# Where TensorE's and ScalarE's hardware loops begin, and where P·V of the last pair stands, in a two-layer decode kernel

## The chip, the cores and the metric

The kernel runs on one core of a Trainium2 chip. A core has TensorE (PE in the profile: matmuls, with the weight loads as a row of their own, PEld), VectorE (DVE), ScalarE (ACT), GpSimd (POOL), and SyncE (SP), which here only starts transfers. Each engine runs its own list of instructions in order and waits on semaphores that the others raise. 16 DMA engines move data from the device's memory (HBM) into the core's on-chip memory (SBUF). TensorE writes to another on-chip memory, PSUM, which the other engines read.

The metric is the device time of one execution in microseconds, the median of several runs.

## The reference, cut to what matters

Two sequences (B = 2) decode one token each. Two layers run one after the other with the same weights and caches: attention A with a residual, then a small MLP block B with a residual.

```python
def _A_ref(x, k_cache, v_cache, wq, wo):          # x: (2, 1, 576), after a layer norm
    q = (x @ wq).reshape(2, 1, 32, 128).transpose(0, 2, 1, 3)
    scores = einsum("bhqd,bhkd->bhqk", q, k_cache) * 128 ** -0.5   # k_cache: (2, 32, 16384, 128)
    p = softmax(scores)
    o = einsum("bhqk,bhkd->bhqd", p, v_cache)
    return o.transpose(0, 2, 1, 3).reshape(2, 1, 4096) @ wo
def _B_ref(x, w1, w2, w3, w4):                    # one token each
    hs = ...      # gelu(layernorm(x) @ w1), shifted along the sequence of length 1, @ w2
    x1 = x + hs
    return x1 + gelu(layernorm(x1) @ w3) @ w4     # 576 -> 4608 -> 576
x = x + A(layernorm(x));  x = x + B(layernorm(x))      # layer 0
x = x + A(layernorm(x));  x = x + B(layernorm(x))      # layer 1
```

All inputs are bf16. For each of the 64 (sequence, head) units, K and V are 16384 x 128 numbers each, 4.2 MB; all of them are 537 MB, and the two layers read them nearly twice over. Nothing is reused within a layer, since each unit has one query.

## The kernel before, in words

**Tiles.** A unit's K lies in SBUF as 128 partitions x 128 rows of 128 numbers. TensorE can only contract over partitions, so half of K is transposed on it: eight 128x128 transposes make a chunk (into one of four PSUM buffers `tps`), ScalarE copies ("evacuates") the chunk into one of three SBUF buffers `kt`, and eight matmuls of two columns give its scores in the PSUM bank `sps`. VectorE does the other half without transposing: it multiplies 16 rows per partition by q, which has been spread over all partitions (`qb`), and sums over the 128 numbers ("a dot": TENSOR_TENSOR, then TENSOR_REDUCE).

**Pairs and singles.** Most units are handled two at a time. `pair` takes one transfer of 8.4 MB ("kk", K of two units, unit 0 on partitions 0 to 63, unit 1 on 64 to 127): 16 chunks on TensorE and ScalarE (`turned`, `evacuate`, `score`; scores trail the transposes by LEAD = 2 chunks), and 8 dots on VectorE beside them. A few units at the start and end of a layer are handled alone by `single` (8 chunks, 4 dots). Layer 0 has 1 single, 30 pairs (of which the last 29 are turns of a hardware loop), 3 singles; layer 1 has three units carried over in SBUF (`carried`), 1 single, 29 pairs (28 turns in the loop), 2 singles.

**q's broadcast.** `pair_diag` (VectorE) writes q of each unit onto a diagonal; `pair_q` multiplies that by a matrix of ones on TensorE and copies the result, q on every partition, to `qb[1]` (two ScalarE copies). They are done for the next pair at the end of a pair; `q_broadcast` is the same for a single.

**The end of a pair.** After the last scores VectorE takes the maxima (three short steps), GpSimd reduces over partitions (L1198), ScalarE scales the maximum and computes four exponentials into the tile `both` (L1201, L1206). In the next pair, after all of its 16 chunks, `pair_pv` multiplies V (a transfer "vv" of 8.4 MB) by these: 256 matmuls on TensorE (L1260), then ScalarE copies the result into `o_acc` (L1264). `pair_l`, behind chunk 8, sums the exponentials.

**What sets the order.** The order on each engine is the order in which the Python code emits operations; `Graph` works out the waits. GpSimd also passes landings on: a `relay` waits on GpSimd's queue for a transfer (POOLq L208 in the profile) and then raises a semaphore for TensorE or VectorE. Since that queue is in order, a relay also waits for GpSimd work ahead of it.

**The loop.** `attention` marks the position of TensorE, ScalarE and VectorE before the second pair, and `Graph.loop` turns everything from there into a hardware loop. So before the change all three engines' bodies run from the first chunk of a pair to the end of that pair. The first pair stands in front of the loop as straight code.

**Transfers.** SP issues them in one order (the store's plan) and waits until the buffer is free. In the loops there are two buffers for kk and one for vv: kk0, kk1, vv0, kk2, vv1, kk3, vv2 and so on. kk(i+2) waits until kk(i) is no longer read; its last reader on TensorE is `pair_q` of that pair, which takes the keys of K for this purpose (`self.pair_q(keys)`). vv(i) waits for ScalarE's copy of `pair_pv` of pair i-1. Since SP goes in order, kk(i+2) also stands behind vv(i).

**Around the loop's start.** `attention` calls `single` with a function `ahead`, which `single` runs at its chunk 0: the diagonals and `pair_q` of the first pair and the broadcast for the first single behind the loop (unit `leave`). After that single's softmax and P·V, GpSimd clears the upper half of `both` (L1019), which pairs need to be zero there. Then come the relays of kk0.

Of the kernel before, what the change touches and what calls it, by code (L numbers as in the profile page):

```python
# [32 lines left out]
class Graph:  # L33
# [74 lines left out]
    def mark(self):  # L108
        return {e: len(self.ops[e]) for e in self.LOOPED}

    def loop(self, first, turns, shift):

        for e, i in first.items():
            self.shift[e][i] = shift
            n = len(self.ops[e]) - i
            assert n % turns == 0, (e, n, turns)
            self.loops[e][i] = (n // turns, turns)

# [218 lines left out]
class KB:  # L337
# [15 lines left out]
    LEAVE = (61, 62)  # L353
    KK = ((0, 2), (0, 4))
    VV = (4, 2)
    TURNS = {("w3", 0): 1, ("w3", 1): 1, ("w3", 2): 1, ("w4", 1): 1, ("w4", 3): 1, ("w4", 6): 1, ("w4", 8): 1,
             ("wq", 0): 1, ("wq", 1): 1, ("wq", 2): 1}

# [637 lines left out]
    def attention(self, l):  # L996
        U = self.U
        self.l_now = l
        o = self.order(l)
        enter, leave = self.ENTER[l], self.LEAVE[l]  # L1000
# [6 lines left out]
        def ahead():  # L1007
            self.pair_diag(o[enter])
            self.pair_q()
            self.pair_column(o[enter])  # L1010
            self.q_broadcast(o[leave], leave, 2)
        self.single(l, s, ahead)
        self.softmax_max(l, s, o[s])
        self.softmax_exp(l, s, o[s])
        self.landed(l, "v", o[s])
        for g in range(4):
            self.pv(l, s, o[s], g)
        self.keep_by_act(l, s)
        self.pool(lambda e: e.memset(self.both[64:, 0, :], 0.0), writes=[*self.both_keys, "cleared"])  # L1019
        firsts = [o[s] for s in range(enter, leave, 2)]  # L1020
        for i, u in enumerate(firsts):
            if i == 1:
                first = self.g.mark()
                self.base = self.chunk
            self.pair(l, i, u, firsts[i - 1] if i else None)
        a, z = self.KK[l]
        self.g.loop(first, len(firsts) - 1, (z - a) * self.TILE // 2)
        self.base = None
        if l == 0:
            self.single(l, leave, lambda: self.q_broadcast(o[leave + 1], leave + 1, 1, [("qb", 1)]))  # L1030
# [23 lines left out]
        u = o[U - 1]  # L1054
# [15 lines left out]
        c = self.place(l, s)  # L1070
        at = 4 * c
        o = self.mps[:, 448:449]
# [4 lines left out]
        i = (self.U - 2) % self.NS  # L1077
# [10 lines left out]
    def single(self, l, s, ahead, top=None, exp=None, pv=None, turn=False):  # L1088
# [4 lines left out]
        for c in range(2 * n):  # L1093
# [6 lines left out]
            self.chunk += 1  # L1100
            while len(pend) > self.LEAD:
                self.scores(*pend.pop(0))
            if c == 0:
                ahead()
            if c % n in (0, 2):
                i = c % n // 2
# [15 lines left out]
    def pair(self, l, i, u, was):  # L1122
# [46 lines left out]
        for c in range(n):  # L1169
            turned(c, self.chunk)  # L1170
            self.evacuate(c, self.chunk)
            pend.append((c, self.chunk))
            self.chunk += 1
            while len(pend) > self.LEAD:
                score(*pend.pop(0))
            if c % 2 == 0:
                dot(c // 2)
            if c == n // 2 and was is not None:
                self.pair_l(was)
        while pend:  # L1180
            score(*pend.pop(0))
        if was is not None:
            self.pair_pv(was)
        self.pair_q(keys)
        self.used(l, nm, 2 * NB)
        m0, m1 = self.mx2[:, 0:1], self.mx2[:, 1:2]
# [7 lines left out]
        for h, (lo, hi) in enumerate(sides):  # L1194
            self.dv(lambda e, h=h, lo=lo, hi=hi: e.tensor_tensor(out=self.mx2[lo:hi, 2 + h:3 + h], in0=m0[lo:hi],  # L1195
                                                                in1=m1[lo:hi], op=ALU.max),
                    reads=["mx2_0", "mx2_1"], writes=["mx2_2"], sig=("mx2", h))
        self.pool(lambda e: e.partition_all_reduce(self.mx2[:, 4:6], self.mx2[:, 2:4], channels=128, reduce_op=ROP.max),  # L1198
                  reads=["mx2_2", "cleared"], writes=["mx2_4"])
        self.pair_column(u + 2)  # L1200
# [2 lines left out]
        for part in (1, 0):  # L1203
            for h, (lo, hi) in enumerate(sides):
# [3 lines left out]
                    bias=self.mx2[lo:hi, 6 + h:7 + h], scale=self.scale, accum_out=self.ls2[lo:hi, part:part + 1]),  # L1208
                    reads=["mx2_6"] + ([("s_dve", 0), ("s_dve", 1)] if part else [("sps", 0)]),
                    writes=[*self.side[h][part], ("lsp", part, h)], sig=("exp", part, h))  # L1210

    def half_scores(self, h):

# [474 lines left out]
```

## Time and profile before

| | us |
|---|---|
| median of 3 runs | 2564.79 (2562.66 to 2565.45) |
| the profiled execution, its own time | 2565.86 |
| its span in the trace | 2564.1 |
| busy: DVE / PE / ACT / POOL | 1903.5 / 1646.0 / 1229.4 / 31.4 |
| HBM read | 1092.37 MB, 426 GB/s over the span |

The page of the profile gives busy time by engine, the span in 40 slices, the transfers by queue, the chain of waits that ended last, and the costliest groups of instructions. Other views are the timeline (instructions in order of time: start, length, engine, line, operation, tiles written and read, count, and in brackets the idle time of that engine before it and what ended it; "issue" is a wait for nothing that the profile shows), and a table by stretches of time (busy time of each engine, TensorE's granted clock, the share of time that the 16 DMA engines were busy, and GB/s). Neighbouring rows of the timeline overlap, since matmuls are pipelined.

### The profile page before, as it was taken

The numbers are of one execution on the slowest core, as the hardware profiler recorded it, in microseconds if no ns is written. First come the engines' busy times: TensorE is split into PE (matmuls) and PEld (weight loads), VectorE is DVE, ScalarE is ACT, GpSimd is POOL, SyncE is SP. The second block draws the span as 40 slices with busy tenths as digits, with TensorE's granted clock in tenths as the row PEclk, the third lists the DMA queues.
The fourth block names the chain that finished last, engine by engine and source line by source line (L and its number), as shares of the span: only waits on it lengthen the run. The fifth ranks groups of instructions, "written<-read, shape, count | busy, mean of one in ns | idle before, by whom it ended". The sixth has DMA issues, their size and how long they took to land.

```text
span 2564.1 us, 82334 instructions
## 1 busy us (share of the span) xinstructions
PE 1646.0 (64%) x34410; PEld 1441.1 (56%) x34410; DVE 1903.5 (74%) x1697; ACT 1229.4 (48%) x1943; POOL 31.4 (1%) x97
## 2 busy tenths in 40 slices
PE   3666576576575575675775775675665665665765
PEld 3555565465565565564665665565555555555655
DVE  4987787787787787788447887777877877877882
ACT  2545355355455454454434554454454454454551
POOL 0000000000000000000000000000000000000000
PEclk8676676676676676676656676676676776676765
DMA  9899999999999999999999899999999999999999
GB/s 413 372 430 440 427 440 427 440 427 440 427 440 427 440 427 440 427 440 419 407 408 419 359 441 426 441 426 441 426 441 426 441 426 441 426 441 426 441 426 384
DMA packets 29942, 1093.30 MB, mean 426 GB/s; under 512 B 3252, under 2 KB 4408, under 8 KB 10552
## 3 DMA queue, kind: packets, MB, share of 16 engines
q1 hardware_dynamic: 29880, 1092.39, 99.0%
q8 instruction: 49, 0.80, 0.1%
q14 instruction: 13, 0.11, 0.0%
HBM read 1092.37 MB, written 0.00 MB: 426 GB/s over the span
## 4 chain that ended last, share of the span: by engine, by line
DMA 73%; PE 18%; issue 6%; ACT 1%; SPq 1%; another core or an unknown queue 0%; DVE 0%; POOL 0%; ACTq 0%; POOLq 0%
DMA mem<-in_A_v_cache_dram 70%; PE mps L1260 16%; DMA mem<-in_B_w_dram 1%; SPq L103 1%; DMA mem<-in_A_k_cache_dram 1%; ACT kt L1466 1%; PE tps L1142 0%; ACT o_acc L1264 0%; PE mps L1588 0%; DMA mem<-in_A_wq_dram 0%; PE sps L1480 0%; DMA mem<-in_A_wo_dram 0%; PE tps L1451 0%; PE mps L919 0%
## 5 line engine op out<-in xcount | busy, mean ns | idle before, releaser
L1142 PE MATMUL tps<-same,mem 128*128 128x128 bf16 x7552 | 948.1, 244 | 575.7 <-POOLq L208 572.0
L1466 ACT ACTIVATE kt<-tps 128x1024 bf16<-128x1024 bf16 x992 | 969.4, 1033 | 358.1 <-PE tps L1142 329.4
L1142 PEld LDWEIGHTS tps<-same,mem 128*128 (+1 forms) x7552 | 688.0, 99 | 745.5 <-issue 583.1
L1167 DVE TENSOR_REDUCE s_dve<-prod 128x16 f32<-128x2048 bf16 x472 | 1078.4, 2285 | 14.2
L1162 DVE TENSOR_TENSOR prod<-mem,qb 128x2048 bf16<-128x2048 bf16 x472 | 578.0, 1224 | 472.7 <-POOLq L208 412.5
L1260 PE MATMUL mps<-both,mem 128*128 128x2 bf16 x15104 | 412.2, 165 | 67.2 <-POOLq L208 62.2
L1260 PEld LDWEIGHTS mps<-both,mem 128*128 128x128 bf16 x15104 | 407.3, 103 | 72.1 <-POOLq L208 67.0
L1153 PE MATMUL sps<-q_col,kt 128*128 128x2 bf16 x7552 | 329.0, 165 | 46.6 <-ACT kt L1466 41.9
L1153 PEld LDWEIGHTS sps<-q_col,kt 128*128 128x128 bf16 x7552 | 289.9, 98 | 60.4 <-ACT kt L1466 46.3
L1264 ACT ACTIVATE o_acc<-mps 128x2 f32 (+1 forms) x59 | 10.2, 173 | 509.0 <-PE mps L1260 509.0
L1201 ACT ACTIVATE mx_<-mx_ 128x2 f32<-128x2 f32 x59 | 12.0, 203 | 169.4 <-POOL mx_ L1198 169.4
L1234 ACT ACTIVATE qb<-sps 64x128 bf16<-64x128 f32 x122 | 33.1, 272 | 123.2 <-PE sps L1228 121.2
L1228 PE MATMUL sps<-diag,same 128*128 128x128 bf16 x61 | 17.6, 288 | 111.6 <-DVE p L1220 111.6
L1451 PE MATMUL tps<-same,mem 128*128 128x128 bf16 x640 | 69.3, 284 | 11.4 <-POOLq L208 11.0
L1498 DVE TENSOR_REDUCE s_dve<-prod 128x16 f32<-128x2048 bf16 x32 | 73.1, 2286 | 1.1
L1228 PEld LDWEIGHTS sps<-diag,same 128*128 128x128 bf16 x61 | 6.4, 106 | 116.4 <-DVE p L1220 116.4
L1451 PEld LDWEIGHTS tps<-same,mem 128*128 128x128 bf16 x640 | 56.1, 130 | 11.8 <-POOLq L208 11.7
L1206 ACT ACTIVATE both<-s_dve,mx_ 64x128 bf16<-64x128 f32 x118 | 47.0, 399 | 2.7
L1198 POOL PARTITION_ALL_REDUCE mx_<-mx_ x59 | 21.0, 355 | 2229.8 <-DVE mx_ L1195 2229.8
L1206 ACT ACTIVATE both<-sps,mx_ 64x128 bf16<-64x128 f32 x118 | 42.8, 362 | 2.3
L1466 ACT ACTIVATE mem<-tps 128x1024 bf16<-128x1024 bf16 x32 | 31.1, 1047 | 19.4 <-PE tps L1451 17.1
L1247 ACT ACTIVATE l<-ls_ 64x1 f32 (+1 forms) x118 | 34.5, 292 | 9.0
(154 smaller groups left out, 545.5 us busy)
## 6 DMA issues: line engine op xcount, KB each, us to landing
mem<-in_A_k_cache_dram SPq DMA_DIRECT2D x6, 4096.0 KB, 39.4
mem<-in_A_v_cache_dram SPq DMA_DIRECT2D x5, 4096.0 KB, 29.2
mem<-in_B_w_dram SPq DMA_DIRECT2D x21, 576.0 KB, 7.7
mem<-in_B_w_dram SPq DMA_DIRECT2D x7, 1152.0 KB, 33.0
mem<-in_A_v_cache_dram SPq DMA_DIRECT2D x3, 2048.0 KB, 44.9
mem<-in_A_wq_dram SPq DMA_DIRECT2D x10, 512.0 KB, 7.0
mem<-in_A_wo_dram SPq DMA_DIRECT2D x8, 576.0 KB, 14.9
mem<-in_A_wq_dram SPq DMA_DIRECT2D x4, 1024.0 KB, 8.0
```

The lines of the kernel that those rows point to most:

```text
L103: sp.dma_start(dst, src).then_inc(h, 16)
L1142: ins = pe.transpose(self.tps[t][:, j * 128:(j + 1) * 128], place(c * CH + j, 1), self.ident[:, :])
L1153: ins = pe.matmul(self.sps[0][:, 2 * b:2 * b + 2], lhsT=kt[:, j * 128:(j + 1) * 128], rhs=self.q_col2[:, :], start=True, stop=True, skip_g ...
L1162: self.dv(lambda e: e.tensor_tensor(out=prod, in0=place(NB + i * DB, DB).rearrange("p (j d) -> p j d", d=128), in1=qbc, op=ALU.mult), read ...
L1167: self.dv(lambda e: e.tensor_reduce(out=self.s_dve2[:, i * DB:(i + 1) * DB], in_=prod, axis=AX.X, op=ALU.add), reads=["prod"], writes=[("s ...
L1206: self.act(lambda e, h=h, lo=lo, hi=hi, src=src, part=part: e.activation(out=self.both[lo:hi, h, NB * part:NB * (part + 1)], in_=src, func ...
L1234: self.act(lambda e, h=h, lo=lo, hi=hi: e.activation(out=self.qb[1][lo:hi, :], in_=qps[lo:hi, 128 * h:128 * (h + 1)], func=ACT.Copy), read ...
L1247: self.act(lambda e, c, lo=lo, hi=hi: e.activation(out=self.l[lo:hi, bass.ds(c, 1)], in_=self.ls2[lo:hi, 0:1], func=ACT.Identity, bias=sel ...
L1260: ins = pe.matmul(self.mps[:, 448:450], lhsT=buf[:, b * 128:(b + 1) * 128], rhs=self.both[:, :, b], start=b == 0, stop=b == 2 * self.NB - ...
L1451: ins = pe.transpose(self.tps[t][:, j * 128:(j + 1) * 128], buf[:, j * 128:(j + 1) * 128], self.ident[:, :])
L1466: self.act(lambda e: e.activation(out=out, in_=self.tps[t][:, :], func=ACT.Copy), reads=[("tps", t)], writes=keys, sig=("evac", c, t, k))
L1498: self.dv(lambda e: e.tensor_reduce(out=sd[:, c0:c0 + DB], in_=prod, axis=AX.X, op=ALU.add), reads=["prod"], writes=[("s_dve", r)], sig=(" ...
```

## The change

Four things are changed; what is computed stays the same, and so does each engine's number of operations.

1. `pair` now returns marks, and `Graph.loop` takes an end as well as a start. VectorE's loop keeps its place. The loops of TensorE and ScalarE begin ahead of `pair_q` (q's broadcast for the next pair), so that a turn runs from the end of pair i-1 (broadcast, scaling of the maximum, exponentials) through the chunks of pair i. The number of turns stays 29 and 28; the end of the last pair is straight code behind the loop.
2. `pair_pv` of the pair before is called behind chunk 12 (PVAT, the 13th of 16), no longer behind the last scores. It takes ScalarE's copy into `o_acc` along.
3. In `single`, `ahead` runs at chunk 4 (`c == n`) instead of chunk 0, in all singles that have one. The broadcast for unit `leave` is taken out of `ahead` and stands behind the whole single.
4. GpSimd's clearing of `both` moves from ahead of the first pair into it, right before that pair's reduction over partitions (only where there is no pair before: `was is None`).

ScalarE around the loop of layer 0, before: copies of chunks into `kt` are L1466, q's copies L1234, the scaling and exponentials L1201 and L1206, `o_acc` L1264; the two L261 rows are the loop's head, REGISTER_ALU and COMPARE_AND_BRANCH its end.

```order
L1466 ACTIVATE kt<-tps 128x1024 x16
L1234 ACTIVATE qb<-sps 64x128 x2
L1201 ACTIVATE mx_<-mx_ 128x2
L1206 ACTIVATE both,ls_<-s_dve,mx_ 64x128 x2
L1206 ACTIVATE both,ls_<-sps,mx_ 64x128 x2
L261 ISA
L261 UNCONDITIONAL_BRANCH
L1466 ACTIVATE kt<-tps 128x1024 x9
```

And now, from the first pair's copies on (line numbers are 3 or 4 higher):

```order
L1470 ACTIVATE kt<-tps 128x1024 x16
L261 ISA
L261 UNCONDITIONAL_BRANCH
L1238 ACTIVATE qb<-sps 64x128 x2
L1204 ACTIVATE mx_<-mx_ 128x2
L1209 ACTIVATE both,ls_<-s_dve,mx_ 64x128 x2
L1209 ACTIVATE both,ls_<-sps,mx_ 64x128 x2
L1470 ACTIVATE kt<-tps 128x1024 x9
```

The loop's head has moved ahead of q's copies. Further down in the same turn ScalarE now has

```order
L1470 ACTIVATE kt<-tps 128x1024 x4
L1268 REGISTER_ALU
L1268 ACTIVATE o_acc<-mps 128x2
L1470 ACTIVATE kt<-tps 128x1024 x3
L261 REGISTER_ALU
L261 COMPARE_AND_BRANCH
```

so the copy into `o_acc` stands behind 13 chunks instead of 16, and the turn ends with three chunks.

TensorE at the end of a turn of layer 0, before (L1153 scores, L1260 P·V, L1228 q's broadcast):

```order
L1153 MATMUL sps<-q_col,kt 128x2 x24
L1260 MATMUL mps<-both,mem 128x2 x256
L1228 MATMUL sps<-diag,same 128x128
L1228 MATMUL sps<-p,same 128x128
L261 REGISTER_ALU
L261 COMPARE_AND_BRANCH
```

And now P·V (L1264) inside the turn, between the scores of chunk 10 and the transposes of chunk 13:

```order
L1142 MATMUL tps<-same,mem 128x128
L1153 MATMUL sps<-q_col,kt 128x2 x8
L1264 MATMUL mps<-both,mem 128x2 x256
L1142 ISA
L1142 MATMUL tps<-same,mem 128x128
```

So three chunks' transposes and five chunks' scores now stand behind P·V. VectorE in the single of layer 1 ahead of the loop, before (L1512 is the last step of the carried units; L1220, L1240, L1407 and L1414 write diagonals and columns of q, L1494 and L1498 are a dot):

```order
L1512 TENSOR_TENSOR mx<-mx 128x1
L1220 TENSOR_SCALAR diag<-same,q_f 128x128
L1220 TENSOR_SCALAR p<-same,q_f 128x128
L1240 CAST q_col<-q_f 128x2
L1407 CAST q_col<-q_f 128x1
L1414 TENSOR_SCALAR diag<-same,q_f 128x128
L1494 TENSOR_TENSOR prod<-mem,both 128x2048
L1498 TENSOR_REDUCE s_dve<-prod 128x16
```

And now:

```order
L1516 TENSOR_TENSOR mx<-mx 128x1
L1498 TENSOR_TENSOR prod<-mem,both 128x2048
L1502 TENSOR_REDUCE s_dve<-prod 128x16
L1498 TENSOR_TENSOR prod<-mem,both 128x2048
L1502 TENSOR_REDUCE s_dve<-prod 128x16
L1224 TENSOR_SCALAR diag<-same,q_f 128x128
L1224 TENSOR_SCALAR p<-same,q_f 128x128
L1244 CAST q_col<-q_f 128x2
```

Two of the single's four dots now stand ahead of the diagonals, and the second diagonal (for `leave`) comes after all four. The diff:

```diff
@@ -108,11 +108,11 @@
     def mark(self):
         return {e: len(self.ops[e]) for e in self.LOOPED}
 
-    def loop(self, first, turns, shift):
+    def loop(self, first, last, turns, shift):
 
         for e, i in first.items():
             self.shift[e][i] = shift
-            n = len(self.ops[e]) - i
+            n = last[e] - i
             assert n % turns == 0, (e, n, turns)
             self.loops[e][i] = (n // turns, turns)
 
@@ -353,6 +353,7 @@
     LEAVE = (61, 62)
     KK = ((0, 2), (0, 4))
     VV = (4, 2)
+    PVAT = 12
     TURNS = {("w3", 0): 1, ("w3", 1): 1, ("w3", 2): 1, ("w4", 1): 1, ("w4", 3): 1, ("w4", 6): 1, ("w4", 8): 1,
              ("wq", 0): 1, ("wq", 1): 1, ("wq", 2): 1}
 
@@ -1008,23 +1009,22 @@
             self.pair_diag(o[enter])
             self.pair_q()
             self.pair_column(o[enter])
-            self.q_broadcast(o[leave], leave, 2)
         self.single(l, s, ahead)
+        self.q_broadcast(o[leave], leave, 2)
         self.softmax_max(l, s, o[s])
         self.softmax_exp(l, s, o[s])
         self.landed(l, "v", o[s])
         for g in range(4):
             self.pv(l, s, o[s], g)
         self.keep_by_act(l, s)
-        self.pool(lambda e: e.memset(self.both[64:, 0, :], 0.0), writes=[*self.both_keys, "cleared"])
+        marks = []
         firsts = [o[s] for s in range(enter, leave, 2)]
         for i, u in enumerate(firsts):
             if i == 1:
-                first = self.g.mark()
                 self.base = self.chunk
-            self.pair(l, i, u, firsts[i - 1] if i else None)
+            marks.append(self.pair(l, i, u, firsts[i - 1] if i else None))
         a, z = self.KK[l]
-        self.g.loop(first, len(firsts) - 1, (z - a) * self.TILE // 2)
+        self.g.loop(marks[0], marks[-1], len(firsts) - 1, (z - a) * self.TILE // 2)
         self.base = None
         if l == 0:
             self.single(l, leave, lambda: self.q_broadcast(o[leave + 1], leave + 1, 1, [("qb", 1)]))
@@ -1100,7 +1100,7 @@
             self.chunk += 1
             while len(pend) > self.LEAD:
                 self.scores(*pend.pop(0))
-            if c == 0:
+            if c == n:
                 ahead()
             if c % n in (0, 2):
                 i = c % n // 2
@@ -1177,10 +1177,11 @@
                 dot(c // 2)
             if c == n // 2 and was is not None:
                 self.pair_l(was)
+            if c == self.PVAT and was is not None:
+                self.pair_pv(was)
         while pend:
             score(*pend.pop(0))
-        if was is not None:
-            self.pair_pv(was)
+        mark = self.g.mark()
         self.pair_q(keys)
         self.used(l, nm, 2 * NB)
         m0, m1 = self.mx2[:, 0:1], self.mx2[:, 1:2]
@@ -1195,6 +1196,8 @@
             self.dv(lambda e, h=h, lo=lo, hi=hi: e.tensor_tensor(out=self.mx2[lo:hi, 2 + h:3 + h], in0=m0[lo:hi],
                                                                 in1=m1[lo:hi], op=ALU.max),
                     reads=["mx2_0", "mx2_1"], writes=["mx2_2"], sig=("mx2", h))
+        if was is None:
+            self.pool(lambda e: e.memset(self.both[64:, 0, :], 0.0), writes=[*self.both_keys, "cleared"])
         self.pool(lambda e: e.partition_all_reduce(self.mx2[:, 4:6], self.mx2[:, 2:4], channels=128, reduce_op=ROP.max),
                   reads=["mx2_2", "cleared"], writes=["mx2_4"])
         self.pair_column(u + 2)
@@ -1208,6 +1211,7 @@
                     bias=self.mx2[lo:hi, 6 + h:7 + h], scale=self.scale, accum_out=self.ls2[lo:hi, part:part + 1]),
                     reads=["mx2_6"] + ([("s_dve", 0), ("s_dve", 1)] if part else [("sps", 0)]),
                     writes=[*self.side[h][part], ("lsp", part, h)], sig=("exp", part, h))
+        return {**self.g.mark(), "tensor": mark["tensor"], "scalar": mark["scalar"]}
 
     def half_scores(self, h):
 
```

## The prediction

> **What bounds the kernel now.** I read the page first, then a table of long and short stretches, then SP's rows and the timeline where the transfers pause. The page:
>
> ```profile
> span 2564.1 us, 82334 instructions
> ...
> q1 hardware_dynamic: 29880, 1092.39, 99.0%
> q8 instruction: 49, 0.80, 0.1%
> ```
>
> The transfers' packets fill 99% of 16 engines' time; no compute engine is near that. So an edit pays only where the DMA engines pause. Stretches (columns: length, then busy time and count of PE, PEld, DVE, ACT, POOL, TensorE's clock, DMA share, GB/s):
>
> ```profile
> 100.00:150.00 50.00, 43.37 (x948) 37.97 (x947) 44.99 (x36) 30.46 (x44) 0.35 (x1) 0.74 0.84 355
> 240.00:1180.00 940.00, 610.67 (x12479) 529.20 (x12480) 723.99 (x582) 467.15 (x729) 8.51 (x24) 0.68 1.00 433
> 1400.00:1450.00 50.00, 36.67 (x661) 31.71 (x662) 46.49 (x41) 30.17 (x51) 0.74 (x2) 0.64 0.78 323
> 1500.00:2430.00 930.00, 601.81 (x12373) 522.25 (x12370) 714.84 (x577) 457.99 (x720) 8.50 (x24) 0.68 1.00 433
> ```
>
> Within the loops the DMA share is 1.00 at 433 GB/s: a transfer of 8.39 MB takes 19.4 us, a pair's two 38.7 us, and nothing can be gained there. At each loop's start a hole is left: 0.16 x 50 = 8.0 us in layer 0 and 0.22 x 50 = 11.0 us in layer 1 (each to about 0.3, from the rounding of the share). 19.0 us is the most that filling both can give.
>
> Why the DMA engines pause: SP has nothing to issue. Layer 0, the second pair, which is the loop's first turn:
>
> ```profile
> 84.38 0.33 SPq L103 DMA_DIRECT2D mem<-in_A_k_cache_dram  x1
> ...
> 84.49 0.58 ACT L1234 ACTIVATE qb<-sps 64x128 bf16<-64x128 f32 x2 [11.44 <-PE sps L1228]
> ...
> 87.69 3.23 PE L1142 MATMUL tps<-same,mem 128*128 128x128 bf16 x24 [3.23 <-POOLq L208]
> ...
> 89.91 0.19 ACT L1206 ACTIVATION_READ_ACCUMULATOR both<-sps,mx_ 64x1 f32 x1
> ...
> 95.72 8.88 ACT L1466 ACTIVATE kt<-tps 128x1024 bf16<-128x1024 bf16 x9 [5.62 <-issue]
> ...
> 110.25 0.23 PE L1142 MATMUL tps<-same,mem 128*128 128x128 bf16 x1 [1.64 <-issue]
> ...
> 114.13 6.97 PE L1260 MATMUL mps<-both,mem 128*128 128x2 bf16 x256
> ...
> 121.21 0.17 ACT L1264 ACTIVATE o_acc<-mps 128x2 f32 x1 [7.37 <-PE mps L1260]
> ...
> 121.41 0.33 SPq L103 DMA_DIRECT2D mem<-in_A_v_cache_dram  x1
> ```
>
> kk2 goes out at 84.38; the next issue, vv1, is at 121.41, 0.20 us behind ScalarE's copy of the first pair's P·V. What was queued at 84.38 (vv0 and kk2) has run out by then. Two waits "issue" lie in this chain: 5.62 us at ScalarE's entry into the loop, 1.64 on TensorE in the middle of chunk 13. Nobody signals them. Behind the first row the Trainium skill, "Runtime: NRT & Kernel Launch", section on instruction fetch, says that a taken branch to code outside the window must fetch it first; that agrees with 5.62 us at the branch.
>
> Layer 1, the same place:
>
> ```profile
> 1403.64 0.33 SPq L103 DMA_DIRECT2D mem<-in_A_k_cache_dram  x1
> ...
> 1406.92 3.32 PE L1142 MATMUL tps<-same,mem 128*128 128x128 bf16 x24 [3.21 <-POOLq L208]
> ...
> 1409.36 8.75 ACT L1466 ACTIVATE kt<-tps 128x1024 bf16<-128x1024 bf16 x9
> ...
> 1421.08 0.34 PE L1153 MATMUL sps<-q_col,kt 128*128 128x2 bf16 x8
> ...
> 1423.56 0.23 PE L1142 MATMUL tps<-same,mem 128*128 128x128 bf16 x1 [1.41 <-issue]
> ...
> 1427.43 6.97 PE L1260 MATMUL mps<-both,mem 128*128 128x2 bf16 x256
> ...
> 1434.71 0.33 SPq L103 DMA_DIRECT2D mem<-in_A_v_cache_dram  x1
> ```
>
> Here ScalarE enters without a stall, and vv1 is still late, at 1434.71. The cause lies earlier, in the single ahead of the loop:
>
> ```profile
> 1356.24 0.25 DVE L1414 TENSOR_SCALAR diag<-same,q_f 128x128 bf16<-128x128 bf16 x1 [8.39 <-PE sps L1228]
> ...
> 1366.04 0.35 PE L1480 MATMUL sps<-q_col,kt 128*128 128x1 bf16 x8 [0.56 <-ACT kt L1466]
> ...
> 1370.86 0.21 DVE L1509 TENSOR_REDUCE mx<-sps 128x1 f32<-128x64 f32 x1
> ...
> 1371.36 0.35 POOL L1514 PARTITION_ALL_REDUCE mx<-mx  x1 [26.52 <-DVE mx L1512]
> ...
> 1376.41 0.31 POOL L1019 MEMSET both<- 64x256 bf16 x1 [4.70 <-PE mps L1588]
> ...
> 1376.52 1.23 DVE L1162 TENSOR_TENSOR prod<-mem,qb 128x2048 bf16<-128x2048 bf16 x1 [5.26 <-POOLq L208]
> ```
>
> VectorE stood 8.39 us before the second diagonal, because `diag` was still to be read by TensorE, which was busy with carried units; so its dots ended 4.5 us behind the last scores (1366.39). Then GpSimd's clearing waited 4.70 us for the single's P·V, and the relay of kk0 behind it let VectorE start the first pair only at 1376.52.
>
> **The change, part by part.**
>
> Loops begun ahead of q's broadcast. ScalarE has nothing to do for 11.44 us before 84.49, when its last chunk of the first pair is done. The branch now falls there, so its 5.62 us lie in that idle time. If ScalarE's new head needed more than 11.44 us, q's copies would come late; that is twice the stall measured. The first evacuation of the second pair then starts at 90.1, when the last exponential is read, rather than 95.72. In layer 1 this gives 0. TensorE's entry (two matmuls ahead of the chunks) falls into the same gap.
>
> P·V behind chunk 12. In layer 1's row the scores of chunk 10 end at 1421.42, 12.06 us behind the first evacuation (1409.36). There P·V can now start: layer 0 at 90.1 + 12.06 = 102.2. It runs 6.97 us. Code loads come on top: the trace shows none of P·V's with the DMA engines busy in a first turn (the old one ran in the hole), so I bound them by P·V as straight code and by the longest such wait:
>
> ```profile
> 1219.17 5.09 PE L1260 MATMUL mps<-both,mem 128*128 128x2 bf16 x185 [7.68 <-POOLq L208]
> 1226.84 2.04 PE L1260 MATMUL mps<-both,mem 128*128 128x2 bf16 x71 [2.58 <-issue]
> ...
> 1352.29 2.83 PE L1588 MATMUL mps<-p,mem 128*128 128x1 bf16 x100 [3.69 <-issue]
> ```
>
> From below nothing, from above 3.69 for each of two: the old wait in chunk 13 stands 24 transposes' code or less from P·V's new start, so it moves into P·V's beginning, and a second falls some 128 matmuls on. I take 1.9 (the 1.64 and a little, since P·V gets there sooner) and 2.58, from the 256-matmul row, which is nearest: 4.5 us. P·V ends at 102.2 + 6.97 + 4.5 = 113.7; with 0.3 from its end to the issue as before (121.10 to 121.41), vv1 goes out at 114.0, 7.4 us earlier. Here the Trainium skill's same section would have it that crossing a block of instructions is mostly hidden; by that rule both waits vanish and each hole closes, 19.0 us in all. The row with 2.58 us contradicts it where 256 matmuls follow each other in 6.97 us.
>
> Behind P·V now stand three chunks' transposes and five chunks' scores; on ScalarE three copies wait for `o_acc`. In the first turn they end about 3.7 us behind 113.7, when VectorE is still at its dots (it began behind TensorE's 87.69 and needs 8 x 3.7 us), so nothing waits for these.
>
> Diagonals and clearing, layer 1. VectorE's dots of the single no longer wait for TensorE; they start right behind the carried units' maximum and end before the scores. The scores' end stays near 1366.4 (fewer matmuls ahead, but two copies of q in ScalarE's middle). The reduction over partitions then starts 4.5 us earlier, at 1366.9, and without the clearing ahead of it the relay of kk0 follows at once, at 1367.3. kk0 has landed by then: kk2 was issued into an idle DMA at 1403.64, so vv0, kk1 and kk0 had ended at about 1403.3, 1383.9 and 1364.5. The first pair's dots start at 1367.5 to 1368.5 instead of 1376.52; I take 8.4 us earlier. VectorE sets the first pair's end, so kk2 (1395.2) and the second pair's start (1398.5) move by as much. From there as in layer 0: first evacuation 1401.0, P·V 1413.0 to 1424.4 with 4.4 of code loads, vv1 at 1424.7, 10.0 us earlier. Nothing runs dry at 1403 any more. The clearing, 0.31 us, lies on GpSimd's queue behind the relays, which wait longer; hidden by the first pair's dots.
>
> Diagonals, layer 0, and the later singles: VectorE starts its dots at k's landing instead of behind TensorE's read of the diagonal, and TensorE waits at chunk 4 for two dots. The single's P·V frees vv0's and kk1's buffers about a microsecond sooner while kk0 is still on the wire, and the first pair waits for kk0, so 0. In the singles behind the loops TensorE and ScalarE lose about 2 us at chunk 4; P·V there waited 7.68 us for V's landing (row of 1219.17), so 0.
>
> The turns in between. In the steady state:
>
> ```profile
> 963.76 0.33 SPq L103 DMA_DIRECT2D mem<-in_A_v_cache_dram  x1
> ...
> 967.58 0.61 DVE L1191 TENSOR_REDUCE mx_<-sps 64x1 f32<-64x128 f32 x2
> ...
> 968.66 0.35 POOL L1198 PARTITION_ALL_REDUCE mx_<-mx_  x1 [38.34 <-DVE mx_ L1195]
> ...
> 975.96 3.25 PE L1142 MATMUL tps<-same,mem 128*128 128x128 bf16 x24 [10.45 <-POOLq L208]
> ...
> 995.17 6.98 PE L1260 MATMUL mps<-both,mem 128*128 128x2 bf16 x256 [0.96 <-POOLq L208]
> ...
> 1002.47 0.33 SPq L103 DMA_DIRECT2D mem<-in_A_v_cache_dram  x1
> 1003.11 0.25 DVE L1220 TENSOR_SCALAR diag<-same,q_f 128x128 bf16<-128x128 bf16 x1
> ```
>
> P·V already waits for V's landing (0.96), so vv's issue does not move: 0. Moved forward, P·V holds TensorE from chunk 13 on until 995.2, and the three late chunks end about 3.7 us behind 1002.15, at 1005.9. VectorE's maximum over scores stood at 967.58 + 38.7 = 1006.3; GpSimd's reduction hardly moves, and it has 7.3 us before the next kk lands (968.66 to 975.96). `pair_q`, which frees kk, comes about 2.3 us later; vv's 19.4 us on the wire cover that.
>
> Sum: 7.4 + 10.0 = 17.4 us. The profiled execution took 2565.86 (span 2564.1 and 1.8 around it), 1.07 above the median, so 2548.5 for it and 2547.4 against the median. I say 2547.5. The most that can be told from no change is about 0.2%, 5 us.
>
> **Rivals.**
>
> (a) Both holes close fully: the code loads are hidden. The 1.64 and 2.58 speak against it, TensorE's earlier entry for it. 2564.8 - 19.0 = 2545.8.
>
> (b) The first turns are slower than that: four loads at the bound of 3.69 instead of 1.9 and 2.5 cost 2 x 3.0 = 6 us more, 2553.4. The single 3.69 row is P·V with the DMA engines busy, as it would be here.
>
> (c) Layer 1's first pair does not start earlier (the single's scores end later, or kk0 lands late): then layer 1 gains 10.0 - 8.4 = 1.6 and the sum is 9.0, 2555.8. Against it stands the 4.70 of the clearing, which goes in any case.
>
> (d) Slower than before: TensorE, held from chunk 13 by V's landing in each of 57 turns, ends the pair too late, so that the relay of the next kk falls behind its landing. That starts when the end moves by over 7.3 us; each us more costs 57 us, and 0.3 us more (7.6) would cancel the gain and turn it: 7.6 to 8 us late give 2565 to 2587. The three late chunks would have to take twice as long as computed (11 us, not 3.7).
>
> (e) The change does nothing: vv1 is held by something else by then. Against it: the row of 121.41 follows the copy by 0.2 us in both layers. 2564.8.
>
> **How the numbers follow.** Forecast 0.50, (a) 0.20, (b) 0.13, (c) 0.08, (d) 0.06, (e) 0.03. The likeliest is the forecast. The range reaches from below (a), 2544.5, over (b) to (c), 2556.0; outside are (d), (e) and a little of each end. Faster by over 0.2%: 0.91; within: 0.03; slower: 0.06.
>
> **What would show it.** Right: vv1 issued near 114 and, on the new time scale (all behind layer 0's hole shifted by 7.4), near 1417; DMA share over 0.95 in both stretches; ScalarE's "issue" of 5 us ahead of q's copies or gone; one or two "issue" rows inside the first P·V of each loop; the clearing behind the relays; 1.00 and 433 GB/s in the loops. What would make the forecast wrong: DMA share below 1.00 in the loops, POOLq waits of TensorE at the chunks' start shrinking to 0, or the first pair of layer 1 starting where it did.

## The result and the profile after

| | before | after |
|---|---|---|
| median, first comparison | 2563.79 us (2562.66 to 2565.45) | 2549.24 us (2547.98 to 2550.45) |
| median, second comparison (the same two kernels, run again) | 2564.75 us (2562.31 to 2567.35) | 2548.06 us (2546.56 to 2549.38) |
| profiled execution of the first, its span | 2565.86 us, 2564.1 us | 2550.45 us, 2548.6 us |

The ratio is 0.9943 with a 95% interval of 0.9925 to 0.996 in the first comparison and 0.9933 (0.992 to 0.9947) in the second: 14.6 and 16.7 us faster. The sum of the prediction was 17.4 us.

The stretches that answer to those shown of before (the table by stretches, same columns), and the transfers' line of the page:

```profile
100.00:150.00 50.00, 38.24 (x863) 34.46 (x862) 44.08 (x35) 25.09 (x38) 0.35 (x1) 0.62 0.99 422
240.00:1180.00 940.00, 606.62 (x12460) 540.89 (x12459) 724.48 (x583) 474.67 (x731) 8.51 (x24) 0.64 1.00 433
1393.00:1443.00 50.00, 39.50 (x717) 34.02 (x717) 44.25 (x33) 33.51 (x53) 0.37 (x1) 0.69 0.98 416
1500.00:2430.00 930.00, 599.42 (x12339) 533.91 (x12339) 714.09 (x577) 465.70 (x720) 8.52 (x24) 0.64 1.00 434
```

```profile
q1 hardware_dynamic: 29880, 1092.39, 99.7%
```

The holes at the loops' starts are nearly shut: the share went from 0.84 to 0.99 and from 0.78 to 0.98. By the rate a little more is missing than by the share: 422 of 433 GB/s over 50 us leaves 1.3 us, 416 leaves 2.0 us. The loops themselves run as before, 1.00 at 433 and 434 GB/s.

The timeline of layer 0's second pair in the kernel after (P·V is L1264 now, the copies into `kt` L1470, q's copies L1238):

```profile
83.94 0.33 SPq L103 DMA_DIRECT2D mem<-in_A_k_cache_dram  x1
84.05 0.58 ACT L1238 ACTIVATE qb<-sps 64x128 bf16<-64x128 f32 x2 [11.26 <-PE sps L1232]
...
89.67 8.79 ACT L1470 ACTIVATE kt<-tps 128x1024 bf16<-128x1024 bf16 x9
...
101.64 0.38 PE L1264 MATMUL mps<-both,mem 128*128 128x2 bf16 x9
...
103.05 3.58 PE L1264 MATMUL mps<-both,mem 128*128 128x2 bf16 x128 [1.03 <-issue]
...
110.34 3.33 PE L1264 MATMUL mps<-both,mem 128*128 128x2 bf16 x119 [3.72 <-issue]
...
113.99 0.33 SPq L103 DMA_DIRECT2D mem<-in_A_v_cache_dram  x1
```

ScalarE's 5.62 us at the loop's entry are gone from the chain (they lie in the 11.26 us ahead of q's copies). The transfers by queue bear this out. They list two queues of the kind instruction, q8 and q14, which we read as the engines' code. The trace does not say which engine a queue serves; the times fit ScalarE for q14. In the kernel before, two packets of q14 start inside the stall, at 92.9 and 94.0; in the kernel after, two start in ScalarE's idle time, at 74.9 and 80.4. P·V begins at 101.64 instead of 114.13. It now holds two waits "issue", 1.03 and 3.72, with exactly 128 matmuls between them. vv1 goes out at 113.99; the forecast was 114.0.

Layer 1, from the single to the loop's first P·V:

```profile
1356.63 0.25 DVE L1418 TENSOR_SCALAR diag<-same,q_f 128x128 bf16<-128x128 bf16 x1 [3.10 <-PE sps L1232]
...
1361.59 0.35 POOL L1518 PARTITION_ALL_REDUCE mx<-mx  x1 [21.36 <-DVE mx L1516]
...
1361.76 1.23 DVE L1162 TENSOR_TENSOR prod<-mem,qb 128x2048 bf16<-128x2048 bf16 x1 [0.27 <-POOLq L208]
...
1366.63 0.31 POOL L1200 MEMSET both<- 64x256 bf16 x1 [4.69 <-PE mps L1592]
...
1388.88 0.33 SPq L103 DMA_DIRECT2D mem<-in_A_k_cache_dram  x1
...
1392.16 3.33 PE L1142 MATMUL tps<-same,mem 128*128 128x128 bf16 x24 [3.21 <-POOLq L208]
...
1394.59 8.79 ACT L1470 ACTIVATE kt<-tps 128x1024 bf16<-128x1024 bf16 x9
...
1406.57 0.38 PE L1264 MATMUL mps<-both,mem 128*128 128x2 bf16 x9
...
1408.22 3.55 PE L1264 MATMUL mps<-both,mem 128*128 128x2 bf16 x128 [1.28 <-issue]
...
1415.52 3.33 PE L1264 MATMUL mps<-both,mem 128*128 128x2 bf16 x119 [3.74 <-issue]
...
1419.16 0.33 SPq L103 DMA_DIRECT2D mem<-in_A_v_cache_dram  x1
```

VectorE's second diagonal comes after the dots, the reduction over partitions and the relay of kk0 follow each other within 0.17 us, and the clearing still waits 4.69 us for the single's P·V, but behind the relay, beside the first pair's dots.

One row of the steady state, SP's issue of a vv in the middle of layer 0's loop:

```profile
996.09 0.33 SPq L103 DMA_DIRECT2D mem<-in_A_v_cache_dram  x1
```

In the kernel before this issue stood at 1002.47. So this issue moved by 6.38 us, where vv1 had moved by 7.42.

### The profile page after: what moved, and what is told of

It reads as the page before. It is cut to its first block, busy times and chain, and to the rows that moved or that the text cites. A ratio compares the mean times of both kernels' runs of the same rounds, so it can differ in the third digit from the quotient of the medians.

```text
span 2548.6 us, 82336 instructions
## 1 busy us (share of the span) xinstructions
PE 1646.1 (65%) x34410; PEld 1478.3 (58%) x34410; DVE 1902.9 (75%) x1697; ACT 1248.4 (49%) x1943; POOL 32.3 (1%) x97
## 4 chain that ended last, share of the span: by engine, by line
DMA 73%; PE 18%; issue 5%; DVE 1%; SPq 1%; ACT 1%; POOL 0%; ACTq 0%; POOLq 0%; DVEq 0%
DMA mem<-in_A_v_cache_dram 68%; PE mps L1264 16%; DMA mem<-in_A_k_cache_dram 3%; DMA mem<-in_B_w_dram 1%; SPq L103 1%; PE tps L1142 1%; DVE s_dve L1502 1%; PE mps L1592 0%; ACT o_acc L1268 0%; DVE prod L1498 0%; PE tps L1455 0%; DMA mem<-in_A_wq_dram 0%; PE sps L1484 0%; DMA mem<-in_A_wo_dram 0%; PE sps L1153 0%
## 5 line engine op out<-in xcount | busy, mean ns | idle before, releaser
L1470 ACT ACTIVATE kt<-tps 128x1024 bf16<-128x1024 bf16 x992 | 987.2, 1026 | 365.1 <-PE tps L1142 336.3
L1142 PEld LDWEIGHTS tps<-same,mem 128*128 (+1 forms) x7552 | 696.5, 108 | 536.2 <-issue 401.9
L1264 PE MATMUL mps<-both,mem 128*128 128x2 bf16 x15104 | 413.1, 165 | 309.6 <-POOLq L208 294.9
L1264 PEld LDWEIGHTS mps<-both,mem 128*128 128x128 bf16 x15104 | 407.8, 103 | 314.9 <-POOLq L208 299.9
L1153 PE MATMUL sps<-q_col,kt 128*128 128x2 bf16 x7552 | 333.0, 166 | 44.4 <-ACT kt L1470 43.0
L1153 PEld LDWEIGHTS sps<-q_col,kt 128*128 128x128 bf16 x7552 | 308.1, 103 | 53.2 <-ACT kt L1470 50.5
L1238 ACT ACTIVATE qb<-sps 64x128 bf16<-64x128 f32 x122 | 33.2, 272 | 100.4 <-PE sps L1232 98.5
L1192 DVE TENSOR_REDUCE mx_<-sps 64x1 f32<-64x128 f32 x118 | 34.0, 288 | 30.0 <-PE sps L1153 27.9
L1201 POOL PARTITION_ALL_REDUCE mx_<-mx_ x59 | 21.0, 355 | 2212.1 <-DVE mx_ L1196 2212.1
L1470 ACT ACTIVATE mem<-tps 128x1024 bf16<-128x1024 bf16 x32 | 31.5, 1033 | 18.3 <-PE tps L1455 16.2
## 6 DMA issues: line engine op xcount, KB each, us to landing
mem<-in_A_wo_dram SPq DMA_DIRECT2D x8, 576.0 KB, 14.6
```

The source lines that it names most:

```text
L1142: ins = pe.transpose(self.tps[t][:, j * 128:(j + 1) * 128], place(c * CH + j, 1), self.ident[:, :])
L1153: ins = pe.matmul(self.sps[0][:, 2 * b:2 * b + 2], lhsT=kt[:, j * 128:(j + 1) * 128], rhs=self.q_col2[:, :], start=True, stop=True, skip_g ...
L1192: self.dv(lambda e, h=h, lo=lo, hi=hi: e.tensor_reduce(out=m1[lo:hi], in_=self.half_scores(h), axis=AX.X, op=ALU.max), reads=[("sps", 0)], ...
L1238: self.act(lambda e, h=h, lo=lo, hi=hi: e.activation(out=self.qb[1][lo:hi, :], in_=qps[lo:hi, 128 * h:128 * (h + 1)], func=ACT.Copy), read ...
L1264: ins = pe.matmul(self.mps[:, 448:450], lhsT=buf[:, b * 128:(b + 1) * 128], rhs=self.both[:, :, b], start=b == 0, stop=b == 2 * self.NB - ...
L1470: self.act(lambda e: e.activation(out=out, in_=self.tps[t][:, :], func=ACT.Copy), reads=[("tps", t)], writes=keys, sig=("evac", c, t, k))
```

## The experiments

Eight kernels. Four take one part of the change back; three set P·V elsewhere; one is the changed kernel again. A table with what the medians and the rows gave, then each one. "vv1" is SP's issue of the second vv in each layer.

| kernel | median us | ratio to before (95%) | vv1, layer 0 | vv1, layer 1 |
|---|---|---|---|---|
| before | 2563.79 / 2564.75 | 1 | 121.41 | 1434.71 |
| after, first comparison | 2549.24 | 0.9943 (0.9925 to 0.996) | 113.99 | 1419.16 |
| loops begin as before | 2552.0 | 0.9957 (0.994 to 0.9974) | 118.56 | 1419.49 |
| P·V behind the last scores | 2557.82 | 0.9979 (0.9969 to 0.9988) | 119.17 | 1427.10 |
| diagonals as before | 2551.07 | 0.996 (0.9946 to 0.9974) | 114.03 | 1419.55 |
| clearing as before | 2552.75 | 0.9958 (0.9944 to 0.9972) | 113.93 | 1421.37 |
| after, second comparison | 2548.06 | 0.9933 (0.992 to 0.9947) | 113.8 | 1416.71 |
| P·V behind chunk 10 | 2547.66 | 0.9932 (0.9918 to 0.9945) | 113.0 | 1417.19 |
| P·V behind chunk 8 | 2545.13 | 0.9925 (0.9911 to 0.9939) | 111.7 | 1412.11 |
| P·V behind chunk 2 | 2544.83 | 0.992 (0.9906 to 0.9933) | 107.3 | 1409.70 |

The four kernels from the loops to the clearing were run beside 15 runs of before with a median of 2563.79 us, the same median as in the first comparison; the last four kernels were run beside nine runs with 2564.75 us. The intervals of the loops, the diagonals and the clearing overlap that of after. But all their runs lie above all nine runs of after: their lowest is 2550.50, after's highest is 2550.45.

**The loops begin where they did.**

```diff
-        return {**self.g.mark(), "tensor": mark["tensor"], "scalar": mark["scalar"]}
+        return self.g.mark()
```

> The changed kernel with the loops of TensorE and ScalarE begun behind the exponentials again, as before; P.V behind chunk 12, the diagonals and the clearing stay changed. Theory (what counts is when vv1 goes out in the first turn of each loop): ScalarE's entry stall of 5.6 us comes back behind the exponentials in layer 0, the first evacuation at about 95.3 instead of 89.67, vv1 near 119 instead of 113.99; layer 1 had no such stall and stays. About 5 us slower than the changed kernel: 2554. Rival (the place of the loop's head is free, since only the code loads inside P.V count): within 1 us of the changed kernel, 2549.

Layer 0 of this kernel:

```profile
93.64 8.88 ACT L1470 ACTIVATE kt<-tps 128x1024 bf16<-128x1024 bf16 x9 [4.13 <-issue]
...
107.68 3.57 PE L1264 MATMUL mps<-both,mem 128*128 128x2 bf16 x128 [1.56 <-issue]
...
114.97 3.28 PE L1264 MATMUL mps<-both,mem 128*128 128x2 bf16 x117 [3.72 <-issue]
...
118.56 0.33 SPq L103 DMA_DIRECT2D mem<-in_A_v_cache_dram  x1
```

The stall is back at ScalarE's entry, 4.13 us here, and vv1 is 4.57 us later than in the kernel after. The mechanism held, but the size did not: the time grew by 2.8 us between the medians, not by 5. Layer 1, where ScalarE has no such stall (no run shows why not), gave part back. The mid-loop issue of layer 0 stands 4.6 us later than in after, the dots of layer 1's first pair begin 2.0 us later (1363.72, now at kk0's landing; in after's profiled execution they had waited for VectorE), and vv1 is 0.33 us later, with P·V's first wait absent.

**P·V behind the last scores.**

```diff
-            if c == self.PVAT and was is not None:
-                self.pair_pv(was)
         while pend:
             score(*pend.pop(0))
+        if was is not None:
+            self.pair_pv(was)
```

> The changed kernel with P.V behind the last scores again. Theory: P.V starts three chunks and five scores later, 6.5 us in both layers, with one or two code loads inside it; vv1 near 119 in layer 0 and 5 us later than in the changed kernel in layer 1: 8 to 10 us slower, 2558. Rival (the code loads are shorter once the DMA engines are idle, so P.V in the hole costs nothing more): 3 to 5 us slower, 2553.

It gave 2557.82 us, 8.6 more than after and inside the theory's 8 to 10: more than half of the whole gain is P·V's place. vv1 of layer 0 is where it was expected; in layer 1 it is 7.9 us later than in after, not 5. The DMA share in 100:150 fell to 0.88. The waits in P·V of this kernel, layer 0, and the stretch around them:

```profile
112.63 3.57 PE L1264 MATMUL mps<-both,mem 128*128 128x2 bf16 x128 [3.73 <-issue]
...
116.91 1.95 PE L1264 MATMUL mps<-both,mem 128*128 128x2 bf16 x67 [0.70 <-issue]
```

```profile
108.00:112.00 4.00, 0.90 (x34) 0.82 (x31) 3.82 (x3) 0.00 (x0) 0.00 (x0) 0.50 1.01 430
112.00:116.00 4.00, 3.37 (x126) 3.37 (x127) 3.70 (x5) 0.00 (x0) 0.00 (x0) 0.50 0.10 37
```

The second wait is 0.70 where it was 3.72: from 112 on the DMA engines are running dry. This is read again below.

**The diagonals as before** (`ahead` at chunk 0, the broadcast for `leave` in it).

```diff
             self.pair_column(o[enter])
+            self.q_broadcast(o[leave], leave, 2)
         self.single(l, s, ahead)
-        self.q_broadcast(o[leave], leave, 2)
...
-            if c == n:
+            if c == 0:
                 ahead()
```

> The changed kernel with the diagonals at chunk 0 of the single and the broadcast for the unit behind the loop inside it again. Theory: in layer 0 nothing; in layer 1 VectorE's dots of the single wait for TensorE again and end 4 us later, so the first pair starts about 3.6 us later (1365.3 instead of 1361.76) and so does vv1: 3 to 4 us slower, 2552.7. Rival (the clearing alone held the first pair): 0, 2549.

The median is 1.8 us above after's, about half of the expected 3 to 4. Its five runs fall into two groups, three at 2550.50 to 2551.07 and two at 2555.22 and 2555.79; the profiled one is of the first. In this kernel the second diagonal stood 7.40 us (8.39 before), and the first pair began as follows:

```profile
1336.47 0.16 DVE L1516 TENSOR_TENSOR mx<-mx 128x1 f32<-128x1 f32 x1
...
1348.21 0.25 DVE L1418 TENSOR_SCALAR diag<-same,q_f 128x128 bf16<-128x128 bf16 x1 [7.40 <-PE sps L1232]
...
1363.08 0.16 DVE L1516 TENSOR_TENSOR mx<-mx 128x1 f32<-128x1 f32 x1
...
1363.50 1.23 DVE L1162 TENSOR_TENSOR prod<-mem,qb 128x2048 bf16<-128x2048 bf16 x1 [0.27 <-POOLq L208]
```

That is only 1.74 us behind the first profiled execution of after (1361.76). But that execution had a late single: its carried units' maximum came at 1338.72, that of after's second profiled execution at 1335.80, with nearly the same arrival from layer 0 (996.09 and 995.64). In the second execution the first pair's dots began at 1358.98:

```profile
1356.23 0.35 POOL L1518 PARTITION_ALL_REDUCE mx<-mx  x1 [18.93 <-DVE mx L1516]
...
1358.98 1.23 DVE L1162 TENSOR_TENSOR prod<-mem,qb 128x2048 bf16<-128x2048 bf16 x1 [2.84 <-POOLq L208]
```

There the relay came 2.4 us behind the reduction, so the wait was for kk0's landing and no longer for VectorE. Against that execution the old diagonals cost 4.5 us at this point and 2.8 at vv1 (1419.55 against 1416.71). What the diagonals do to VectorE is clear when counted from the carried units' maximum (the first L1516 row above) to the single's (the second): 26.6 us here and 26.9 in the kernel before, but 20.2 to 22.9 in the eight profiled executions with the diagonals at chunk 4. So the single's maximum comes 3.7 to 6.4 us sooner, where about 4 were expected. How much of that reaches the time depends on when the single starts and when kk0 lands: by the rows 0.4 to 2.8 us at vv1, by the median 1.8, and more in two runs of five. How much of it is the part and how much the spread of the single's start is not settled.

**The clearing as before.**

```diff
         self.keep_by_act(l, s)
+        self.pool(lambda e: e.memset(self.both[64:, 0, :], 0.0), writes=[*self.both_keys, "cleared"])
...
-        if was is None:
-            self.pool(lambda e: e.memset(self.both[64:, 0, :], 0.0), writes=[*self.both_keys, "cleared"])
```

> The changed kernel with GpSimd's clearing ahead of the first pair again. Theory: in layer 1 the relay of kk0 waits for the single's P.V again, the first pair's dots start at 1366.7 instead of 1361.76 and vv1 goes out 5 us later: 4 to 5 us slower, 2553.9; in layer 0 nothing. Rival (VectorE catches up, since TensorE and ScalarE start the first pair behind that P.V in any case): 0 to 1 us.

Measured 2552.75 us, 3.5 more than after, where 4 to 5 were expected. The relay stood behind the clearing again (which ran at 1365.73, after 4.69 us for the single's P·V), the first pair's dots began at 1365.84, 4.1 us later than in after, and kk2 went out at 1392.95, again 4.1 later. At vv1 only 2.2 of it were left: P·V, which came later, had no first wait.

**The changed kernel again, and P·V earlier.** The last four differ in one number:

```diff
-    PVAT = 12
+    PVAT = 10
```

and 8 and 2.

> The changed kernel again, beside the three that follow, so that they are compared on the same chip: 2549 us, vv1 near 114.0 in layer 0 and near 1419 in layer 1.

> P.V of the last pair behind chunk 10 instead of 12, all else as in the changed kernel. Theory (what is left of the two holes, some 1.4 us in layer 0 and 2.2 us in layer 1, is there because vv1 is issued late): two chunks of 1.04 us each fewer ahead of P.V, vv1 2.1 us earlier in each layer (111.9 and, with what layer 0 gives, near 1415.5), 2 to 3 us shorter, 2546 to 2547. Rival (code loads: TensorE stalls longer at P.V's blocks the sooner it gets there, so the gain is given back as waits 'issue' in P.V): vv1 within 0.7 us of 114.0, 2549.

> P.V behind chunk 8. Theory: vv1 4.2 us earlier than in the changed kernel, both holes filled, 3.6 us shorter (2545.6), DMA share 0.99 to 1.00 in the stretches 100:150 and 1393:1443. In the loops the last scores end 4.1 us later than with 12, GpSimd's reduction still ends ahead of k's landing (margin there 6.9 us): 38.70 us a turn as before. Rival (code loads eat it): 2548 to 2549.

> P.V behind chunk 2, so that TensorE stands still from chunk 3 on until V lands. The last scores end 10.3 us later than with 12, more than the 6.9 us that GpSimd's reduction has before the next k lands: the relay falls 3 to 4 us behind k's landing in each turn. The prediction's rival (d) prices this at 57 turns times the lateness: 57 x 3.4 = 194 us slower, about 2743. Theory against that price: a pair that starts late loses nothing, since its P.V waits for V's landing in any case and SP issues the next k some 8 to 12 us before the DMA engines would run dry; so the lateness does not add up from turn to turn: 2545.6 as with 8, with the DMA share at 1.00 in the loops and TensorE's and VectorE's wait for the relay released by GpSimd behind its reduction. If only part of it comes through (say VectorE's dots end too late), something between.

The changed kernel again gave 2548.06 us; its vv1 in layer 1 went out at 1416.71 and not near 1419. P·V of the first turn in layer 0, behind chunk 10 and then behind chunk 8:

```profile
99.43 1.44 PE L1264 MATMUL mps<-both,mem 128*128 128x2 bf16 x49
102.87 3.58 PE L1264 MATMUL mps<-both,mem 128*128 128x2 bf16 x128 [1.99 <-issue]
110.43 2.27 PE L1264 MATMUL mps<-both,mem 128*128 128x2 bf16 x79 [3.99 <-issue]
```

```profile
97.34 2.51 PE L1264 MATMUL mps<-both,mem 128*128 128x2 bf16 x89
102.88 3.57 PE L1264 MATMUL mps<-both,mem 128*128 128x2 bf16 x128 [3.03 <-issue]
110.17 1.20 PE L1264 MATMUL mps<-both,mem 128*128 128x2 bf16 x39 [3.72 <-issue]
```

Behind chunk 10 the rival was the better one, though vv1 moved a little more than its 0.7 us: P·V starts 2.2 us sooner than in the kernel after, the first wait grows from 1.03 to 1.99 and the last part begins at 110.43, no earlier than after's 110.34. vv1 gains 0.8 us, which is no more than the shorter last part (79 matmuls in 2.27 us, not 119 in 3.33), and the median is the same as that of after within what can be told. Behind chunk 8 both were half right: P·V starts 4.3 us sooner, the first wait is 3.03, and the last part still begins at 110.17; vv1 is 2.1 us earlier and not 4.2. The time fell all the same, to 2545.13 us, near the 2545.6 of the theory: both holes are shut.

Stretches of the kernel with P·V behind chunk 8, and then behind chunk 2:

```profile
100.00:150.00 50.00, 37.64 (x801) 34.39 (x801) 43.98 (x34) 25.77 (x38) 0.35 (x1) 0.60 1.00 427
...
1393.00:1443.00 50.00, 37.79 (x836) 34.86 (x835) 44.23 (x33) 26.34 (x39) 0.37 (x1) 0.60 1.00 429
```

```profile
100.00:150.00 50.00, 37.19 (x775) 33.78 (x771) 39.51 (x31) 25.63 (x38) 0.36 (x1) 0.60 1.00 431
240.00:1180.00 940.00, 597.15 (x12339) 531.70 (x12336) 724.79 (x583) 450.63 (x722) 8.54 (x24) 0.64 1.00 433
1393.00:1443.00 50.00, 31.79 (x730) 28.70 (x731) 40.08 (x31) 20.75 (x32) 0.37 (x1) 0.60 1.00 431
```

Behind chunk 2, vv1 goes out 4.4 us sooner than behind chunk 8 in layer 0 and nothing more is gained (2544.83 against 2545.13): there is no hole left to fill. This kernel is also the test of rival (d). A turn of it:

```profile
955.71 0.33 SPq L103 DMA_DIRECT2D mem<-in_A_v_cache_dram  x1
...
970.95 0.33 SPq L103 DMA_DIRECT2D mem<-in_A_k_cache_dram  x1
...
971.16 0.36 POOL L1201 PARTITION_ALL_REDUCE mx_<-mx_  x1 [38.22 <-DVE mx_ L1196]
971.32 3.23 PE L1142 MATMUL tps<-same,mem 128*128 128x128 bf16 x24 [0.29 <-POOLq L208]
...
987.08 6.99 PE L1264 MATMUL mps<-both,mem 128*128 128x2 bf16 x256 [11.71 <-POOLq L208]
...
994.41 0.33 SPq L103 DMA_DIRECT2D mem<-in_A_v_cache_dram  x1
```

P·V waits 11.71 us for V, whose landing is at 987.1; k, one transfer of 19.4 us ahead of it, had landed at about 967.7 (an estimate; its last landing in the trace is at 967.64). GpSimd's reduction ends the pair at 971.16 and the next pair starts right behind it, 3.6 us late. It happens in each turn, and the turn is still 38.70 us (955.71 to 994.41). At 57 us for each us of lateness, as (d) had it, this kernel would have been some 200 us slower. So lateness at the end of a pair does not add up here: P·V of the next pair waits for V's landing in any case, and with it SP's next vv; and the k issued at 970.95 still goes out while vv (issued at 955.71, on the wire until 987.1) has 16 us to run. The prediction named POOLq waits shrinking to 0 as a sign that its forecast would be wrong; here they shrank to 0.29 us and cost nothing.

Behind chunk 2 the kernel beats the changed one: its runs lie between 2544.03 and 2545.42 us, and none of the nine of after lies below 2546.56. Behind chunk 8 the median says the same (2545.13), though its runs reach to 2547.45. Both are faster than the kernel before by 19.6 to 19.9 us, which is about what the two holes held (19.0 by the share).

## Why the prediction was right, and which terms were off

The direction and mechanism held: the gain is the two holes, and the pace of the loops did not change. The forecast of 2547.5 us stands 1.7 below the first median and 0.6 below the second.

- *ScalarE's entry.* Right. First evacuation forecast at 90.1, measured 89.67; taking the part back brought a stall of 4.13 us and vv1 4.57 us later.
- *P·V's place.* Right. Forecast start 102.2, measured 101.64 (the profiled execution runs 0.44 us ahead from kk2 on).
- *P·V's code loads.* Slightly low: 4.5 taken in layer 0 and 4.4 in layer 1, measured 1.03 + 3.72 = 4.75 and 1.28 + 3.74 = 5.02. The division was wrong: the second wait is not the 2.58 of the single's row but the 3.7 of the bound, and the first is smaller than the 1.9 taken. That the two errors nearly cancel is luck. So rival (b) was right on the second wait and wrong on the first. Rival (a), hidden loads, was refuted; that its time (2545.8) was nearly reached with P·V behind chunk 8 is due to reaching the loads sooner, not to their being hidden.
- *vv1 in layer 0.* Right, 114.0 and 113.99. The step that failed is the next one, "all behind layer 0's hole shifted by 7.4". From vv1 to the vv row in mid-loop it took 881.06 us before (121.41 to 1002.47) and 882.10 after (113.99 to 996.09), 1.04 us more; in the second execution 0.75 more. The restart of the transfers did not lose this. The trace has 16 signals for a landing, as many as there are DMA engines, and P·V, and with it the next vv, waits for the last one. Of the V that this row waited for, the middle of the 16 signals is at 994.41 before and 987.32 after, 7.1 us earlier; the last is at 995.08 and 988.69, 6.4 earlier. So most of the data kept the lead, and the last signals came later behind the others.
- *Layer 1's first pair.* Right at the point forecast: 8.4 us earlier was taken, and 1376.52 less the 6.38 that arrived from layer 0 less 8.4 is 1361.74; measured 1361.76. To the point this is luck: it needed the late single of that execution. The first evacuation (1394.59) and P·V's start (1406.57) follow the forecast in the same way (1401.0 and 1413.0 less 6.38). In the second profiled execution the pair began 2.8 us earlier than that, at kk0's landing.
- *vv1 in layer 1.* Forecast near 1417, measured 1419.16 and, in the second execution, 1416.71. By its steps: 10.0 us forecast for this layer, 15.55 - 6.38 = 9.2 measured in the first; 0.6 of the difference is the code loads. The issue rows behind it lag again: from vv1 to the vv issue of the turn at 1991.82 it took 572.66 us, against 571.44 before (1967.45 less 1434.71, plus one turn of 38.70). In the second execution it is 1.1 more.
- *Sum.* The 17.4 us were forecast for the profiled execution, and that one became 15.4 us shorter (2565.86 to 2550.45). 17.4 less 1.04 (layer 0's issue row) and 0.8 (vv1 in layer 1) is 15.6. The lag of layer 1's issue rows is not in this sum, since it did not reach the end: vv1 of layer 1 stood 15.55 us earlier than before, and the span ended 15.5 earlier (2564.1 to 2548.6). In the second execution it is 18.0 and 17.5, with its earlier start of layer 1's first pair. The medians differ by 14.6 and 16.7.
- *Diagonals in the singles, clearing, turns in between.* Costed at nothing where hidden, and the loops bear it out. Rival (c) fell: the first pair did start earlier. Rival (e) fell.
- *Rival (d).* It did not occur, since the margin was 6.9 us by the profile after, and its price was wrong: with P·V behind chunk 2 the margin was overrun by 3.6 us in each turn without cost.

Why the 16 signals of a landing lie further apart in the loop after (1.52 us from the first to the last, 0.82 before) stays open. With the loops begun as before they lie 2.03 us apart, and from vv1 to mid-loop it took 882.15 us, although the engines had stood still ahead of that vv1 (DMA share 0.89 in 100:150). So it does not come from an issue that just meets the end of the last transfer. Behind chunk 2 they lie 3.03 us apart, behind chunk 8 2.42: with vv1 4.4 us earlier the mid-loop issue is no earlier (994.41 against 994.33).

## What to carry to other kernels

Where transfers set the time, look at the places where their queue runs dry, find what the late issue waited for, and give back every part of that chain; an issue that barely meets the end of the last transfer still leaves a gap, so aim some microseconds ahead of it (here the first packet of vv1 started 0.96 us behind its issue, 1.3 us were missing by the rate with vv1 at 113.99, and with vv1 at 111.7 the share was 1.00). In these kernels an engine's first pass through long straight code stalled block by block, so starting it earlier gained only what the blocks allowed. In these loops, bound by landings, work that ended late did not add up from turn to turn while the next issue still fell within the transfer in flight; price such a delay against that slack before calling it a slope.

## What the runs showed that was not expected

- *Code arrives at a rate.* Between P·V's two block starts in a first turn lie 7.29 us in after (103.05 to 110.34), 7.30 in its layer 1, 7.29 with the loops as before (107.68 to 114.97), 7.56 behind chunk 10 and 7.29 behind chunk 8, wherever P·V began (97.34 to 105.69). The 128 matmuls themselves take 3.58. So with the DMA engines busy a block of 128 matmuls and their 128 weight loads came once in 7.3 us. The trace shows the packets: in after's layer 0 those of the queue q8, 16 KB each, start at 100.50, 107.83 and 114.14, and the three waits "issue" of TensorE there end 2.4 to 2.6 us later, at 103.05, 110.34 and 116.56 (the third lies behind P·V). With the engines running dry the step of the block starts was 4.28 us (P·V behind the last scores: 112.63 to 116.91), and the packets started 3.92 us apart (110.27 and 114.19). This contradicts, for such code, what the Trainium skill states in "Runtime: NRT & Kernel Launch", section on instruction fetch, that crossing a block is mostly hidden. That the DMA load is the cause is argued from these two cases; no run changed it alone.
- *No such wait in later turns*: with 256 matmuls in each, the steady rows of P·V carry only V's landing, as at 987.08 above. The transfers by queue of the kernel after say the same. First from 100 to 117 us, in the loop's first turn, then from 126 to 1200 us, the turns behind it, where no packet of q8 is left:

```profile
q8 instruction: 3, 0.05, 1.2%
```

```profile
q1 hardware_dynamic: 8049, 464.59, 100.0%
q14 instruction: 1, 0.01, 0.0%
```

- *The same kernel's layer 1 starts 2 to 3 us apart* in two profiled executions (carried maximum at 1338.72 and 1335.80), more than the difference some of the experiments were to show.
